# Three of seven recurrence batches on 16x16 blocks, with block layouts changed by VectorE transposes, in a fused delta-rule and SoLU kernel

## The chip, the core and the metric

The kernel runs on one core of one Trainium2 chip. The metric is the device time of a whole execution in microseconds (us), median over runs. A profiled execution also has a span, from its first to its last instruction, and a trace whose times count from the start of that span.

## The reference

A delta rule runs over 768 tokens for 4 batches times 8 heads with dimension 48; what it gives goes, row by row, through a small feed-forward layer.

```python
k_n = k / (norm(k) + 1e-6)
for t in range(S):                                   # S = 768
    kt, vt, bt = k_n[:, :, t], v[:, :, t], beta[:, :, t, None]
    y[:, :, t] = einsum('bhd,bhde->bhe', q[:, :, t], state)
    v_old = einsum('bhde,bhd->bhe', state, kt)
    state = state + bt[..., None] * einsum('bhd,bhe->bhde', kt, vt - v_old)
x = y.transpose(0, 2, 1, 3).reshape(B * S, H * D)    # 3072 x 384
h = x @ w_in                                         # 384 x 1024
solu = h * softmax(h)
ln = (solu - mean) / sqrt(var + 1e-6) * g_ln
out = ln @ w_out                                     # 1024 x 384
```

## The kernel before, in words

The 768 steps are cut into 12 chunks of 64 tokens. A **unit** is one chunk of one pair of batches (128 partitions: two batches of 64 tokens; 8 heads in the free direction). There are 24 units, worked in the order 0 to 23. Inside a chunk the 64 steps are replaced by a triangular system: with G the Gram matrix of the chunk's keys, a lower triangular matrix is inverted, and the result T (tile `zt`) is applied by TensorE. So a unit goes: `gram` and `qk` on TensorE (line 498), T ready, then the `chain` (line 649): `kps` from the state, `r` on VectorE (DVE), `ups` from T and r, `u` on ScalarE (ACT), `cps` and `yps`, the state; then `moe_h` (line 709: `h` on TensorE, softmax on DVE and ACT, tiles `pr`, `ph`, `pl`), then `moe_out` (line 759: `ops`, `oc`). Here "u of unit 10" is the ACT copy that follows the unit's `ups`.

T is made for several units at once, in seven **batches** m: m=0 has units 0 and 1, m=1 to 5 have four each (2 to 5, 6 to 9, 10 to 13, 14 to 17, 18 to 21), m=6 the last two. For a batch:

- `gram` copies G to SBUF (ACT, tile `g`) and sends it to DRAM (`gd`).
- `to_inv` reads it back with another layout into `ginv`: one partition holds one 32x32 diagonal block of one unit and head, so that 128 blocks lie side by side. `norms` takes the key norms from its diagonal (18 small DVE instructions), `inv_begin` scales it (two 128x1024 DVE instructions and a select on GpSimd, POOL), the start of the tile `y`.
- `inv_step` is the recurrence that inverts a 32x32 block: 30 steps, each one multiply (`itmp`) and one add (`y`). For m=0 and 1 a step is split: columns 0 to 9 on DVE, the rest on POOL. For m>1 all of it is on POOL. The select that opens a batch on POOL ("the select of m=3") and the last `y` bound the batch there.
- `inv_end` has ACT turn a copy of the block round and sends both through DRAM (`zd`, `xd`) into the layout that TensorE needs: `zt`, `gx` and `gy`. Eight DMAs, all in SP's queue, which also holds every other transfer.
- `block_level` puts two 32x32 blocks together to 64x64 (TensorE `mps`, ACT `msb`, TensorE, ACT).

The weights come as 8-byte numbers. `to_f32` turns them to 32-bit ones with DVE, ACT and POOL, and they are kept as a high and a low half each (`win_hi`, `win_lo`, `wout_hi`, `wout_lo`): six pieces of w_in and eight of w_out. `column_sums` (TensorE tile `cs`) needs all of w_out, and stands ahead of the first `ops` on TensorE.

The order of every engine's instructions is set when the program is built: a recorder gives every instruction a cost and a due time, runs through them once by these numbers (`order`), and emits each engine's list. An engine works its list strictly in order. For example, a DMA is costed so, and the batches' due times are written out:

```python
return self.rec.add(self.name, self.engine.dma_start, (), kw, kb * 5.0, 2000)
tn = e - 5.4 if m > 1 else -10.8
add(inversion(m, tn + 0.6, e - 2.6 if m > 1 else -10))
```

Of the kernel before, what the change touches and what calls it, by code (L numbers as in the profile page):

```python
# [305 lines left out]
def kernel(  # L306
# [190 lines left out]

    def gram(m, u, t0):
# [8 lines left out]
        if m == 2:  # L507
            rec.after = last0[0]
        for h2 in range(0, H, 2):
            with rec.atomic():  # L510
                for h, b2 in hb[2 * h2 : 2 * h2 + 4]:
                    pe.matmul(
                        ns=60, out=gps_[half(1 - b2), h], lhsT=k[dims(b2), h, 0], rhs=k[dims(b2), h, 0],
                        start=True, stop=True,
                    )
                    pe.matmul(
                        ns=60, out=pps[half(b2), h], lhsT=k[dims(b2), h, 0], rhs=k[dims(b2), h, 1],
                        start=True, stop=True,
                    )
        rec.after = None  # L520
        act.copy(out=g, in_=gps_)
# [7 lines left out]
    ginv, yt = {}, {}  # L529
    last0 = [None]  # L530

    def to_inv(m):
        gi = p2.tile([P, 32, 32], F32, tag="ginv", name=f"ginv_{m}")
        ginv[m] = gi
        for b in range(4):
            blk = b % 2
            for z in range(1 if len(units(m)) == 4 else 2):
                src = gdt[m].rearrange("t u h j -> t (u h) j")
                n = H * len(units(m))
                ls = slice(0, n)  # L540
                sp.dma_start(
                    kb=128, out=gi[32 * b + 16 * z : 32 * b + 16 * z + n],
                    in_=src[32 * b : 32 * b + 32, ls, blk * 32 : blk * 32 + 32].rearrange("j l i -> l j i"),
                )

    def inv_begin(m):
        gi, nn, nb = ginv[m], nnt[m], bb[m]
        full = [P, 32, 32]
# [12 lines left out]
    def inv_step(m, j):
        y, b = yt[m], ginv[m]
        n = 31 - j
        parts = [(gps, 0, j)] if m > 1 else [(dve, 0, min(j, 10)), (gps, 10, j)]
        for eng, c0, c1 in parts:
            if c1 <= c0:
                continue
            c = c1 - c0
            tmp = p1.tile([P, 256], F32, tag=f"itmp{eng.name}", name=f"itmp_{m}_{j}_{c0}")
            tv = tmp[:, 0 : c * n].rearrange("p (c i) -> p c i", i=n)  # L570
# [4 lines left out]
            eng.tensor_tensor(out=y[:, c0:c1, j + 1 : 32], in0=y[:, c0:c1, j + 1 : 32], in1=tv, op=ALU.add)

    def inv_end(m):
        y, x1 = yt[m], ginv[m]
# [12 lines left out]
        for b in range(4):
# [3 lines left out]
            sp.dma_start(kb=128, out=zz[rows, 0:n, blk * 32 : blk * 32 + 32], in_=zd[r0 : r0 + n].rearrange("l j i -> j l i"))  # L595
            if blk == 0:
                for t, r1 in ((xx, r0), (xy, r0 + 32)):
                    sp.dma_start(kb=128, out=t[r1 : r1 + 32, 0:n], in_=xd[r0 : r0 + n].rearrange("l j i -> j l i"))
# [328 lines left out]
```

## Time and profile before

| what | value |
|---|---|
| median of 3 runs | 512.82 us (512.18 to 515.02) |
| profiled execution, its own time | 512.04 us |
| its span | 510.2 us, mean granted TensorE clock 0.920 |
| busy: TensorE, DVE, ACT, POOL | 368.2, 318.6, 192.9, 294.0 us |
| chain that ended last | POOL 28%, PE 22%, DVE 19%, issue 10%, DMA 9%, SP's queue 7% |

The busy times are sums over the whole span. Nearly all instructions are recorded by one helper, so all have line L265, and they are told apart by tile names. In a timeline row stand the start, the duration, the engine, the tiles written and read and the shape; a row of the windows gives for a stretch of time the busy time of each engine, with the number of instructions in brackets. "SPq" is the issuing of a DMA by SP.

### The profile page before, as it was taken

How to read it: one execution, taken by the hardware profiler on the slowest of the kernel's cores; microseconds unless marked ns; L12 is line 12 of the kernel's file. 1: busy time of each engine (PE TensorE's matmuls, PEld its weight loads, DVE VectorE, ACT ScalarE, POOL GpSimd, SP SyncE). 2: the span in 40 equal slices, each digit the busy share in tenths (PEclk: the TensorE clock that was granted, in tenths of full speed). 3: DMA queues.
4: the chain of work that ended last, by engine and by line, in shares of the span. 5: the costliest groups of instructions: out<-in, count | busy, mean ns of one | idle time of the engine just before them, and what ended most of it. 6: DMA issues, size and time to landing. Idle time of an engine off the chain costs nothing.

```text
span 510.2 us, 18246 instructions
## 1 busy us (share of the span) xinstructions
PE 368.2 (72%) x7744; PEld 233.9 (46%) x7744; DVE 318.6 (62%) x791; ACT 192.9 (38%) x382; POOL 294.0 (58%) x506
## 2 busy tenths in 40 slices
PE   3510070689579488997598997787969797899974
PEld 3410070455346345665366564444635464566532
DVE  3599999887884383655088664256597355455670
ACT  2210241465522143536144544224345345454450
POOL 3378385966558998984016886008989898100000
PEclk9999999877876699998799998898989899999998
DMA  8685662987989949977999587985656866744332
GB/s 212 159 255 98 155 169 65 161 171 174 172 162 165 179 113 160 168 135 161 189 165 144 145 162 151 160 162 95 107 118 144 145 114 128 131 64 99 73 68 61
DMA packets 180640, 72.21 MB, mean 142 GB/s; under 512 B 165520, under 2 KB 168976, under 8 KB 180560
## 3 DMA queue, kind: packets, MB, share of 16 engines
q1 hardware_dynamic: 180560, 71.06, 70.8%
q8 instruction: 60, 0.98, 0.9%
q14 instruction: 20, 0.16, 0.1%
HBM read 37.21 MB, written 16.52 MB: 105 GB/s over the span
## 4 chain that ended last, share of the span: by engine, by line
POOL 28%; PE 22%; DVE 19%; issue 10%; DMA 9%; SPq 7%; ACT 4%; POOLq 0%; DVEq 0%; ACTq 0%
POOL y L265 13%; POOL itmp L265 11%; PE h L265 7%; SPq L265 7%; PE ops L265 7%; DVE y L265 5%; DVE itmp L265 4%; DMA zt<-zd 3%; DMA ginv<-gd 3%; PE mps L265 2%; DVE wf L265 2%; DVE rst L265 1%; DVE st L265 1%; PE kps L265 1%; PE yps L265 1%
## 5 line engine op out<-in xcount | busy, mean ns | idle before, releaser
L265 POOL TENSOR_TENSOR y<-y,itmp 128x84 f32<-128x84 f32 (+16 forms) x190 | 100.7, 530 | 14.6
L265 POOL TENSOR_TENSOR itmp<-y,ginv 128x84 f32<-128x84 f32 (+16 forms) x190 | 93.3, 491 | 14.0
L265 DVE TENSOR_REDUCE st<-h 128x1 f32<-128x1024 f32 x24 | 29.3, 1222 | 87.5 <-PE h L265 82.2
L265 PE MATMUL qk<-kq 48*64 48x64 f32 x768 | 40.4, 269 | 24.9 <-DVE pm L265 15.6
L265 PE MATMUL gram<-kq 48*64 48x64 f32 x768 | 43.2, 270 | 18.8 <-DMA kq<-kq_dram 11.5
L265 POOL TENSOR_TENSOR st<-st,nhalf 128x1 f32<-128x1 f32 x24 | 13.2, 551 | 64.1 <-DVE st L265 64.1
L265 PEld LDWEIGHTS gram<-kq 48*64 48x64 f32 x768 | 37.5, 178 | 25.7 <-ACT g L265 6.3
L265 PEld LDWEIGHTS <-pth 128*128 128x128 f16 x384 | 37.6, 99 | 25.5 <-issue 1.7
L265 PE MATMUL h<-win_hi,xtl 128*128 128x512 f16 x144 | 45.4, 419 | 5.3 <-DVE pr L265 2.6
L265 PE MATMUL mps<-zt,gx 32*32 32x32 f32 x768 | 13.5, 205 | 48.6 <-issue 28.9
L265 PE MATMUL h<-win_lo,xth 128*128 128x512 f16 x144 | 46.7, 421 | 1.7 <-POOL win_lo L265 1.7
L265 PEld LDWEIGHTS qk<-kq 48*64 48x64 f32 x768 | 35.8, 178 | 25.3 <-DVE pm L265 16.1
L265 PEld LDWEIGHTS <-xth 128*128 128x128 f16 x288 | 28.4, 105 | 39.7 <-issue 14.8
L265 PE MATMUL ops<-wout_hi,ptl 128*128 128x384 f16 x192 | 38.7, 345 | 8.7 <-DMA ptl<-pl 6.8
L265 PE MATMUL h<-win_hi,xth 128*128 128x512 f16 x144 | 43.4, 411 | 0.0
L265 ACT ACTIVATE e<-h,st 128x1024 f32<-128x1024 f32 x24 | 26.7, 1114 | 38.0 <-DVE st L265 26.4
L265 POOL TENSOR_SCALAR_AFFINE_SELECT y<-y 128x1024 f32<-128x1024 f32 x7 | 9.4, 1346 | 53.5 <-DVE y L265 53.5
L265 DVE TENSOR_SCALAR st<-st 128x1 f32<-128x1 f32 (+1 forms) x216 | 35.5, 165 | 5.6
L265 PE MATMUL ops<-wout_lo,pth 128*128 128x384 f16 x192 | 36.9, 334 | 0.0
L265 PEld LDWEIGHTS mps<-zt,gx 32*32 32x32 f32 x768 | 10.1, 117 | 56.9 <-issue 34.8
L265 PE MATMUL ops<-wout_hi,pth 128*128 128x384 f16 x192 | 35.5, 326 | 0.0
L265 PE MATMUL cps<-u,kv 64*64 64x48 f32 x704 | 28.9, 235 | 9.1 <-ACT u L265 3.2
(94 smaller groups left out, 860.4 us busy)
## 6 DMA issues: line engine op xcount, KB each, us to landing
kq<-kq_dram SPq DMA_DIRECT2D x48, 192.0 KB, 4.5
kv<-kv_dram SPq DMA_DIRECT2D x24, 384.0 KB, 4.3
gd<-g SPq DMA_DIRECT2D x48, 128.0 KB, 3.3
out_dram<-oc SPq DMA_DIRECT2D x24, 192.0 KB, 2.2
zd<-y SPq DMA_DIRECT2D x7, 512.0 KB, 2.6
wi<-w_in_dram SPq DMA_DIRECT2D x6, 512.0 KB, 4.4
wo<-w_out_dram SPq DMA_DIRECT2D x8, 384.0 KB, 4.0
ginv<-gd SPq DMA_DIRECT2D x20, 128.0 KB, 4.2
```

What stands on the lines that cost most here:

```text
L265: fn(*[real(a) for a in args], **{k: real(a) for k, a in kw.items()})
```

## The change

For the batches m=0, 1 and 2 (`SPLIT = 3`):

- `gram` makes three 32x32 products per head in place of one 64x64, and ACT copies G's diagonal blocks to `gc` and its lower block straight to `gx`; nothing goes to DRAM. `to_inv` is one DVE transpose of `gc` into `ginv`.
- The recurrence runs on the two 16x16 diagonal blocks of each 32x32 block: 14 steps, the upper block on DVE and the lower on POOL, at the same time.
- `inv_end` is two DVE transposes of 128x1024 (into `zt` and `gy`), a small ACT copy and POOL memsets; no DMA.
- `small_level` is new: per unit 32 plus 32 TensorE matmuls (`sps`), an ACT scaling (`ssb`), a DVE add into `zt`, two DVE transposes of 32x256 into `gx` and two ACT copies, ahead of `block_level`.

For all batches: G goes to DRAM in one DMA per unit where there were two; the last batch's blocks are read in four DMAs, not eight; the two 16-bit halves of x (`xh`, `xl`, now one tile `x`) are transposed by one DMA, not two. The recorder's cost of a DMA has a floor, and due times and precedences of the first batches are changed.

```diff
+SPLIT = 3
...
-        return self.rec.add(self.name, self.engine.dma_start, (), kw, kb * 5.0, 2000)
+        return self.rec.add(self.name, self.engine.dma_start, (), kw, max(550.0, kb * 5.0), 2000)
...
-        return self.rec.add(self.name, self.engine.dma_start_transpose, (), kw, kb * 5.0, 2000)
+        return self.rec.add(self.name, self.engine.dma_start_transpose, (), kw, max(1400.0, kb * 5.0), 2500)
...
     def gram(m, u, t0):
...
+        near = m < SPLIT
+        if near and u == 0:
+            gct[m] = p2.tile([P, 32, 32], F32, tag="y", name=f"gc_{m}")
...
+                        for r, a, b, o in ((0, lo, lo, lo), (32, up, up, lo), (32, up, lo, up)):
+                            pe.matmul(
+                                ns=25, out=gps_[C * b2 + r : C * b2 + r + 32, h, o], lhsT=kk[:, a], rhs=kk[:, b],
+                                start=True, stop=True,
+                            )
...
+            act.copy(out=gct[m][:, hs], in_=gps_[:, :, lo])
+            for r in (32, 96):
+                act.copy(out=gxt[m][0][r : r + 32, hs], in_=gps_[r : r + 32, :, up])
...
-        for b2 in range(2):
-            sp.dma_start(kb=128, out=gdt[m][half(b2), u], in_=g[half(1 - b2)])
+        sp.dma_start(kb=256, out=gdt[m][:, u], in_=g)
...
     def to_inv(m):
...
+        if m < SPLIT:
+            dve.transpose(ns=1900, out=gi.rearrange("l j i -> l i j"), in_=gct[m].rearrange("j l i -> j i l"))
...
+    def blocks(m):
+        return [(dve, slice(0, 16)), (gps, slice(16, 32))] if m < SPLIT else [(gps, slice(0, 32))]
...
     def inv_step(m, j):
-        parts = [(gps, 0, j)] if m > 1 else [(dve, 0, min(j, 10)), (gps, 10, j)]
+        for eng, q in blocks(m):
+            y, b = yt[m][:, q, q], ginv[m][:, q, q]
+            n = q.stop - q.start - 1 - j
...
     def inv_end(m):
+        if m < SPLIT:
+            xy = p1.tile([P, 1040], F32, tag="gy", name=f"gy_{m}")
+            gps.memset(xy[:, 1024:1040], 0.0)
+            act.copy(n=256, out=x1[:, 0:16, 16:32], in_=y[:, 0:16, 0:16].rearrange("p i j -> p j i"))
+            for q in (0, 16):
+                gps.memset(x1[:, q : q + 16, q : q + 16], 0.0)
+            dve.transpose(ns=1900, out=zz[:, :, 32:64].rearrange("p l i -> p i l"), in_=y.rearrange("l j i -> l i j"))
+            dve.transpose(
+                ns=1900, out=xy[:, 0:1024].rearrange("p (l i) -> p i l", i=32), in_=x1.rearrange("l j i -> l i j"),
+            )
+            return
...
+    def small_level(u, nm, zz, z0, gx, xy):
+        t = ps_f.tile([P, 2, H, 32], F32, tag="fl", name=f"sps_{nm}")
+        mps, zps = t[:, 0, :, 0:16], t[:, 1, :, 0:16]
...
+                    pe.matmul(ns=25, out=mps[r, l], lhsT=xy[r, x : x + 32], rhs=zz[r, z0 + l, 48:64], start=True, stop=True)
+        ssb = p1.tile([P, H, 16], F32, tag="msb4", name=f"ssb_{nm}")
+        act.mul(out=ssb, in_=mps, mul=-1.0)
...
+                    pe.matmul(ns=25, out=zps[r, l], lhsT=xy[r, x : x + 32], rhs=ssb[r, l], start=True, stop=True)
+        dve.tensor_tensor(out=zz[:, zs, 48:64], in0=zz[:, zs, 48:64], in1=zps, op=ALU.add)
+        for r in lanes[::2]:
+            dve.transpose(out=gx[r], in_=zz[r, zs, 32:64])
+        for r in lanes[::2]:
+            act.copy(out=zz[r, zs, 0:32], in_=zz[r, zs, 32:64])
...
-        for x, s in ((xl, "l"), (xh, "h")):
-            t = p2.tile([P, 3, P], F16, tag=f"xt{s}", name=f"xt{s}_{nm}")
-            sp.transpose(kb=96, out=t, in_=x)
-            xt[ch, bp].append(t)
+        t = p2.tile([P, 6, P], F16, tag="xt", name=f"xt_{nm}")
+        sp.transpose(kb=192, out=t, in_=x2.rearrange("p a f -> p (a f)"))
...
-        tn = e - 5.4 if m > 1 else -10.8
+        tn = e - 5.4 if m > 1 else -12.99
```

How the instructions stand now, at three places. The last number in a name only tells tiles of one name apart; those of the two kernels are counted apart.

**The end of m=0 on DVE.** Before, the last step of the recurrence (`itmp_30`) is followed by a unit's mask product `pm` and by the norms of m=1 (`rst`, `nrn`):

```order
L265 TENSOR_TENSOR itmp_29_0_612<-y_388,ginv_321 128x20
L265 TENSOR_TENSOR y_388<-y_388,itmp_29_0_612 128x10x2
L265 TENSOR_TENSOR itmp_30_0_616<-y_388,ginv_321 128x10
L265 TENSOR_TENSOR y_388<-y_388,itmp_30_0_616 128x10
L265 TENSOR_TENSOR pm_1_620<-qk_1_417,mask 128x512
L265 TENSOR_SCALAR rst_625<-ginv_553 128x32
L265 TENSOR_SCALAR nrn_627<-rst_625 128x32
```

Now, with `wf` a piece of w_in on its way to 32 bits:

```order
L266 TENSOR_TENSOR itmp_14_0_626<-y_390,ginv_317 128x14
L266 TENSOR_TENSOR y_390<-y_390,itmp_14_0_626 128x14
L266 TENSOR_TENSOR pm_0_631<-qk_0_484,mask 128x512
L266 TENSOR_SCALAR wf_0_639<-wi_0_400 128x512
L266 TENSOR_SCALAR g_sb<-g_sb 128x8
L266 SCALAR_TENSOR_TENSOR wf_0_639<-wi_0_400,wf_0_639 128x512 x2
L266 TENSOR_SCALAR wf_1_726<-wi_1_472 128x512
L266 STREAM_TRANSPOSE zt_229<-y_390 128x32x32
L266 STREAM_TRANSPOSE gy_213<-ginv_317 128x32x32
L266 TENSOR_TENSOR pm_1_745<-qk_1_645,mask 128x512
L266 STREAM_TRANSPOSE ginv_783<-gc_392 128x32x32
```

Behind the recurrence now stand a weight piece and three transposes, the third of which opens m=1.

**m=2 on POOL.** Before, its select (`y_1918`) and its 30 steps stand ahead of the remaining w_out pieces (`wg`, `wc_o`), all rows on POOL:

```order
L265 TENSOR_TENSOR wg_1657<-wg_1657,wc_o_1614 128x384
L265 TENSOR_SCALAR wc_o_1772<-wc_o_1772,g_sb 128x384
L265 TENSOR_TENSOR st_0_1267<-st_0_1267,nhalf 128x1
L265 TENSOR_TENSOR st_0_1267<-st_0_1267 128x1
L265 AFFINE_SELECT y_1918<-y_1918 128x1024
L265 TENSOR_TENSOR wg_1767<-wg_1767,wc_o_1688 128x384
L265 TENSOR_TENSOR itmp_1_0_1984<-y_1918,ginv_1770 128x30
L265 TENSOR_TENSOR y_1918<-y_1918,itmp_1_0_1984 128x30
```

Now POOL scales its half itself and does the small steps:

```order
L266 TENSOR_TENSOR wg_1983<-wg_1983,wc_o_1919 128x384
L266 TENSOR_SCALAR wc_o_2082<-wc_o_2082,g_sb 128x384
L266 MEMSET y_2265 128x16x16 x2
L266 TENSOR_TENSOR ginv_2250<-ginv_2250,nn_2294 128x16x16
L266 TENSOR_TENSOR y_2265<-ginv_2250,nb_2292 128x16x16
L266 AFFINE_SELECT y_2265<-y_2265 128x16x16 x2
L266 TENSOR_TENSOR itmp_1_16_2330<-y_2265,ginv_2250 128x14
L266 TENSOR_TENSOR y_2265<-y_2265,itmp_1_16_2330 128x14
```

POOL's share of m=2 is cut to small instructions; the other half is in DVE's list.

**The opening of m=3, on DVE, and its way back through SP's queue.** Before, m=3's `y` stands on DVE ahead of the softmax of unit 3 (`h_1_2132`) and of the `r` of unit 5 (`r_1_2529`):

```order
L265 TENSOR_TENSOR ginv_2308<-ginv_2308,nn_2417 128x1024
L265 TENSOR_TENSOR y_2431<-ginv_2308,nb_2411 128x1024
L265 SCALAR_TENSOR_TENSOR oc_0_2461<-csum,st_0_1267,ops_0_2415 128x384
L265 TENSOR_REDUCE st_1_2473<-h_1_2132 128x1
L265 TENSOR_SCALAR st_1_2473<-st_1_2473 128x1
L265 SCALAR_TENSOR_TENSOR st_1_2473<-st_1_2473 128x1
L265 TENSOR_SCALAR st_1_2473<-st_1_2473 128x1 x4
L265 SCALAR_TENSOR_TENSOR pr_1_2512,st_1_2473<-h_1_2132,e_1_2491 128x1024
L265 SCALAR_TENSOR_TENSOR oc_1_2522<-csum,st_1_1712,ops_1_2465 128x384
L265 TENSOR_TENSOR r_1_2529<-kv_1_1915,kps_1_2201 128x384
```

Now it stands behind the softmax of unit 3 (`pl_1_3201`), the small level of unit 7 (`sps_1_3205`) and the `r` of unit 6 (`r_0_3351`):

```order
L266 SCALAR_TENSOR_TENSOR pl_1_3201<-pr_1_3169,st_1_3130,ph_1_3183 128x1024
L266 SCALAR_TENSOR_TENSOR oc_0_3272<-csum,st_0_2567,ops_0_3158 128x384
L266 TENSOR_SCALAR st_1_3130<-st_1_3130 128x1
L266 RECIPROCAL nxb_3280<-nrn_3077 128x32
L266 TENSOR_TENSOR nxb_3280<-nxb_3280 128x32
L266 TENSOR_TENSOR nb_3283<-nxb_3280,bt 128x32
L266 TENSOR_SCALAR nn_3285<-nb_3283 128x32
L266 TENSOR_TENSOR ginv_2940<-ginv_2940,nn_3285 128x1024
L266 TENSOR_TENSOR zt_229<-zt_229,sps_1_3205 128x8x16
L266 STREAM_TRANSPOSE gx_1196<-zt_229 32x256 x2
L266 TENSOR_TENSOR r_0_3351<-kv_0_2104,kps_0_3238 128x384
L266 TENSOR_TENSOR y_3359<-ginv_2940,nb_3283 128x1024
```

In SP's queue, before, from m=3's `gy` to its last `zt`:

```order
L265 DMA gy_3421<-xd_3316 32x32x32
L265 DMA_TRANSPOSE xth_0_3431<-xh_0_3417 128x3x128
L265 DMA gx_2399<-xd_3316 32x32x32
L265 DMA gd_2357<-g_0_3436 64x512 x2
L265 DMA_TRANSPOSE pth_0_3464<-ph_0_3444 128x8x128
L265 DMA_TRANSPOSE xtl_0_3476<-xl_0_3459 128x3x128
L265 DMA_TRANSPOSE ptl_0_3491<-pl_0_3467 128x8x128
L265 DMA gy_3421<-xd_3316 32x32x32
L265 DMA zt_278<-zd_3296 32x32x32
```

and now:

```order
L266 DMA gy_4225<-xd_4138 32x32x32
L266 DMA zt_312<-zd_4123 32x32x32 x2
L266 DMA gx_3041<-xd_4138 32x32x32
L266 DMA gd_3607<-g_0_4252 128x512
L266 DMA_TRANSPOSE pth_0_4283<-ph_0_4260 128x8x128
L266 DMA_TRANSPOSE ptl_0_4295<-pl_0_4279 128x8x128
L266 DMA_TRANSPOSE xt_0_4326<-x_4_0_4227 128x6x128
L266 DMA gy_4225<-xd_4138 32x32x32
L266 DMA zt_312<-zd_4123 32x32x32
```

A unit's transposes still stand ahead of the last `zt`, with one transpose and one DMA fewer. From m=4 on the selects stand at the same units as before: m=4 behind the u of unit 10, m=5 between those of units 14 and 15, m=6 just ahead of that of unit 17.

More of the change, by code (lines that the diff above doesn't have):

```diff
@@ L511, in gram @@
                 for h, b2 in hb[2 * h2 : 2 * h2 + 4]:
[L512 to L521, printed above, removed]
+                    kk = k[dims(b2), h, 0]
+                    if near:
+                        for r, a, b, o in ((0, lo, lo, lo), (32, up, up, lo), (32, up, lo, up)):
[3 more added lines that the diff above has]
+                            )
+                    else:
+                        pe.matmul(ns=60, out=gps_[half(1 - b2), h], lhsT=kk, rhs=kk, start=True, stop=True)
+                    pe.matmul(ns=60, out=pps[half(b2), h], lhsT=kk, rhs=k[dims(b2), h, 1], start=True, stop=True)
+            rec.hold(pm)
+        if near:
+            hs = slice(H * u, H * u + H)
+            act.copy(out=gct[m][:, hs], in_=gps_[:, :, lo])
+            for r in (32, 96):
+                act.copy(out=gxt[m][0][r : r + 32, hs], in_=gps_[r : r + 32, :, up])
+        else:
+            act.copy(out=g, in_=gps_)
         dve.tensor_tensor(out=pm, in0=pps, in1=mask.unsqueeze(1).to_broadcast([P, H, C]), op=ALU.mult)
+        if near:
+            return
         if u == 0:
             gdt[m] = dr.tile([P, 4, H, C], F32, tag="gd", name=f"gd_{m}")
-        for b2 in range(2):
-            sp.dma_start(kb=128, out=gdt[m][half(b2), u], in_=g[half(1 - b2)])
-    ginv, yt = {}, {}
-    last0 = [None]
+        sp.dma_start(kb=256, out=gdt[m][:, u], in_=g)
+        moved[m] = rec.ops[-1]
+    ginv, yt, moved = {}, {}, {}
     def to_inv(m):
@@ L534, in to_inv @@
         ginv[m] = gi
+        if m < SPLIT:
+            dve.transpose(ns=1900, out=gi.rearrange("l j i -> l i j"), in_=gct[m].rearrange("j l i -> j i l"))
+            moved[m] = rec.ops[-1]
+            return
+        if len(units(m)) == 2:
+            rec.after = moved[m]
+            dve.memset(gi, 0.0)
+            rec.after = None
+        n = H * len(units(m))
+        src = gdt[m].rearrange("t u h j -> t (u h) j")
         for b in range(4):
             blk = b % 2
[L537 to L544, printed above, removed]
+            r = 32 * (b ^ 2)
+            sp.dma_start(
+                kb=4 * n, out=gi[32 * b : 32 * b + n],
+                in_=src[r : r + 32, 0:n, blk * 32 : blk * 32 + 32].rearrange("j l i -> l j i"),
+            )
@@ L557, in inv_begin @@
         act.copy(n=32, out=y.rearrange("p j i -> p (j i)")[:, 0 : 32 * 32 : 33], in_=nb)
-        yt[m] = y
     def inv_step(m, j):
-        y, b = yt[m], ginv[m]
-        n = 31 - j
-        parts = [(gps, 0, j)] if m > 1 else [(dve, 0, min(j, 10)), (gps, 10, j)]
[L565 to L570, printed above, removed]
+        for eng, q in blocks(m):
+            y, b = yt[m][:, q, q], ginv[m][:, q, q]
+            n = q.stop - q.start - 1 - j
+            if n <= 0:
+                return
+            tmp = p1.tile([P, 256], F32, tag=f"itmp{eng.name}", name=f"itmp_{m}_{j}_{q.start}")
+            tv = tmp[:, 0 : j * n].rearrange("p (c i) -> p c i", i=n)
@@ L621, in block_level @@
         msb = p1.tile([P, n, 32], F32, tag=f"msb{n}", name=f"msb_{nm}")
-        act.mul(out=msb, in_=mps, mul=-1.0)
+        for r in [slice(0, P)] if len(groups) > 1 else [slice(C * b2, C * b2 + 32) for b2 in range(2)]:
+            act.mul(out=msb[r], in_=mps[r], mul=-1.0)
         yield t1
@@ L641, in tlevel @@
         gx, gy = gxt[m]
-        gx, gy = (x[:, H * u : H * u + H] for x in (gx, gy))
+        gx = gx[:, H * u : H * u + H]
+        if m < SPLIT:
+            small_level(u, f"{m}_{u}", ztx[m], H * u, gx, gy)
+            yield from block_level(u, f"{m}_{u}", ztx[m], H * u, [(range(8), gx, gx, 0)], t0, t1)
+            return
+        gy = gy[:, H * u : H * u + H]
         yield from block_level(u, f"{m}_{u}", ztx[m], H * u, [(range(4), gx, gx, 0), (range(4, 8), gx, gy, 32)], t0, t1)
@@ L828 @@
     for i in range(8):
-        add(load_w_out(i, -1 + 0.05 * i, 2.1 + 0.05 * i))
+        add(load_w_out(i, -0.6 + 0.05 * i, 2.1 + 0.05 * i))
     add(once(2.49, column_sums))
```

98 lines of the change are left out of this document (60 added, 38 removed).

## The prediction

> **What bounds the kernel now.** I read the page first: the chain that ended last, then the slices.
>
> ```profile
> POOL 28%; PE 22%; DVE 19%; issue 10%; DMA 9%; SPq 7%; ACT 4%; POOLq 0%; DVEq 0%; ACTq 0%
> DVE  3599999887884383655088664256597355455670
> POOL 3378385966558998984016886008989898100000
> ```
>
> No engine carries the chain alone; a slice is 12.8 us. DVE is nearly full in slices 2 to 6 (26 to 89 us), POOL in slices 12 to 14 (153 to 191 us). So the limit changes, and I went to the timeline where it does: the opening of m=3.
>
> ```profile
> 182.93 1.36 DVE L265 TENSOR_TENSOR y<-ginv,nb 128x1024 f32<-128x1024 f32 x1
> 187.86 1.61 POOL L265 TENSOR_TENSOR kv<-kv,nrt 128x384 f32<-128x384 f32 x2
> 189.43 1.26 POOL L265 TENSOR_SCALAR_AFFINE_SELECT y<-y 128x1024 f32<-128x1024 f32 x1
> 230.46 0.35 SPq L265 DMA_DIRECT2D zd<-y  x1
> 232.95 0.34 SPq L265 DMA_DIRECT2D out_dram<-oc  x1
> 240.89 1.21 SPq L265 DMA_DIRECT2D gd<-g  x2
> 242.20 1.33 SPq L265 DMA_TRANSPOSE pth<-ph  x1
> 243.63 1.36 SPq L265 DMA_TRANSPOSE xtl<-xl  x1
> 247.03 0.60 SPq L265 DMA_DIRECT2D zt<-zd  x1
> 250.75 0.64 PE L265 MATMUL mps<-zt,gx 32*32 32x32 f32 x30 [5.44 <-DMA zt<-zd]
> 265.66 0.48 ACT L265 COPY u<-ups 128x384 f32<-128x384 f32 x1 [1.62 <-PE ups L265]
> 270.88 1.26 POOL L265 TENSOR_SCALAR_AFFINE_SELECT y<-y 128x1024 f32<-128x1024 f32 x1 [4.95 <-DVE y L265]
> ```
>
> DVE had m=3's `y` ready at 184.3; POOL took it only at 189.43, because m=2 and the two `kv` scalings were ahead of it. Then comes a chain without slack: POOL's 30 steps (41.0 us, 189.43 to 230.46), the way through DRAM (20.3 us to PE's `mps` at 250.75, where PE stood 5.44 us for the last `zt`), and 14.9 us to the u of unit 10. The select of m=4 follows that u by 5 us. So the span is 189.4 + 41.0 + 20.3 + 14.9, and 244.6 from u of unit 10 to 510.2. The last term stays, but for the merged DMAs: in both orders the selects of m=4 to 6 hang on the same units, and POOL's 30 steps of m=3 to 6 are untouched. The change is decided by when m=3's select comes.
>
> **What the change does to POOL and DVE before that select.** The recurrences alone (tile `itmp`; columns: stretch, length, DVE busy, POOL busy, clock, DMA), then all of DVE:
>
> ```profile
> 0.00:189.00 189.00, 42.46 (x120) 61.58 (x140) 0.87 0.77 160
> 144.00:189.00 45.00, 0.00 (x0) 33.94 (x60) 0.73 0.81 151
> 0.00:20.00 20.00, 8.61 (x28) 1.00 0.83 207
> 20.00:88.00 68.00, 60.10 (x154) 1.00 0.60 145
> 88.00:189.00 101.00, 73.50 (x156) 0.76 0.87 161
> 0.00:189.00 189.00, 142.21 (x336) 0.87 0.77 160
> ```
>
> The prices:
>
> ```profile
> 30.54 0.22 DVE L265 TENSOR_TENSOR itmp<-y,ginv 128x58 f32<-128x58 f32 x1
> 32.31 0.32 DVE L265 TENSOR_TENSOR itmp<-y,ginv 128x130 f32<-128x130 f32 x1
> L265 DVE TENSOR_TENSOR itmp<-y,ginv 128x210 f32<-128x210 f32 x2 | 0.9, 432 | 0.1
> L265 DVE TENSOR_TENSOR y<-ginv,nb 128x1024 f32<-128x1024 f32 x7 | 8.7, 1238 | 0.2
> L265 ACT COPY ginv<-y 128x1024 f32<-128x1024 f32 x7 | 13.8, 1972 | 50.1 <-issue 19.8 <-POOL y L265 18.5 <-DVE y L265 11.7
> L265 DVE STREAM_TRANSPOSE nrt<-nrn 128x32 f32<-128x32 f32 x7 | 1.4, 207 | 0.1
> 32.90 0.28 POOL L265 TENSOR_TENSOR itmp<-y,ginv 128x54 f32<-128x54 f32 x1
> L265 POOL TENSOR_TENSOR itmp<-y,ginv 128x240 f32<-128x240 f32 x10 | 7.0, 701 | 0.7
> 253.64 3.85 SPq L265 DMA_DIRECT2D ginv<-gd  x4
> ginv<-gd SPq DMA_DIRECT2D x20, 128.0 KB, 4.2
> ```
>
> POOL first. m=2 cost it 33.9 us of steps; now 28 steps of at most 64 elements at 0.28 are 7.8, with the scaling, memsets and selects of its own half, five passes of 256 elements at 0.70, some 11. So POOL is ready long before m=3, and DVE's `y` is what its select waits for. DVE's work up to there:
>
> - removed: the 120 instructions of m=0 and 1, −42.5; six scalings of 128x1024 become 128x256, 6 x (1.24 − 0.43) = −4.9 (0.43 from the row of 210 elements).
> - added: 3 x 28 steps of at most 64 elements x 0.21 (the 0.22 row, most are smaller) = +17.6.
> - added: nine transposes of 128x1024. The trace has none. From below 1.24, a DVE instruction of as many elements; from above 1.97, ACT's copy that turns each block round. I take 1.8, nearer the copy that strides, since DVE's small transpose (0.207) is no cheaper than its small products: 9 x 1.8 = +16.2; 11.2 to 17.7.
> - added: small levels of units 0 to 7, which stand ahead of m=3's `y`: an add (0.30, from the row of 130 elements) and two transposes of 32x256 (0.43 each, as for 210 elements): 8 x 1.16 = +9.3. If 32 partitions cost a quarter, it were 4; if a strided one costs double, 16.
> - moved: m=3's `y` behind the softmax of one more unit, an `oc` and an `r`: +4 (two 128x1024 passes of 1.24, the rest about 1.5).
>
> Sum: 142.2 − 42.5 − 4.9 + 17.6 + 16.2 + 9.3 + 4 = 141.9. DVE's load hardly falls; the halves taken from POOL's m=2 and the transposes eat what the short recurrence frees.
>
> How fast DVE gets through it: the first 20 us hold 8.6, as before (loads). The other 133.3 go at the density DVE shows where nothing bigger holds it, 60.1 of 68 us (88%, 20 to 88 us), rather than at the 73.5 of 101 (73%) of the stretch in which POOL was late anyway: 133.3 / 0.88 = 151.5, so 171.5. Two waits come on top. In m=0 DVE scales its half and then stands for POOL, which scales and selects its own (about 3.5, those five passes); the steps and unit 0's `pm` queue behind. And the norms of m=3 wait for G through DRAM, four issues (3.85) and 4.2 to land, less the small level beside it, about 6.5; `y` and POOL's select queue behind. Together 10: m=3's select at about 181, 8.4 earlier than 189.4.
>
> Covered, at nothing: the small levels' 64 matmuls per unit, about 1.3 us by the 30 `mps` in 0.64, and some four short ACT copies. PE has 91 of the 189 us free:
>
> ```profile
> 0.00:189.00 189.00, 97.60 (x2280) 0.87 0.77 160
> ```
>
> Were the cover gone at units 8 and 9, which come between the select and m=3's `mps`, it costs 2.6. POOL's memsets fall in the time it gains. SP loses all eight DMAs of m=0 to 2, which were not in m=3's way.
>
> **Behind the select.** POOL's 41.0 stays. In the way through DRAM, the rows show what stood between `zd` and the last `zt`: an `out_dram` with its wait (2.1 from the end of `zd`'s issue), now behind `xd`; two `gd`, now one (−0.6); two transposes of x, now one. That issue takes 1.36 for three 128-wide blocks and 1.33 for eight (`pth`), so size does not count and one goes whole, −1.3. 20.3 − 4.0 = 16.3. On the same chain of m=4 and m=5 one `gd` and one transpose go each, −2 each; m=6, with the last units' work over it, nothing.
>
> Span 510.2 − 8.4 − 4.0 − 4 = 493.8; with the 1.84 between span and time of that execution 495.6. It stands 0.8 below the median of the runs: **496 us**.
>
> **Rivals.** *DVE is denser, or the transposes cost 1.24:* 128.3 of work at 88% gives 165.8 + 10 = 176 (time 491); with 92% and half the waits 164.5 (480). For it: DVE has a weight piece to do whenever a step waits. *DVE is sparser:* the mean of both stretches,
>
> ```profile
> 20.00:189.00 169.00, 133.59 (x309) 0.86 0.76 154
> ```
>
> is 79%, 133.3 / 0.79 = 168.7, waits contained in it: select at 188.7, span 501.5, time 504. What I take, 88%, comes from a stretch of back-to-back recurrences; now steps on two engines, levels and softmaxes alternate.
>
> *No change:* the gain behind the select is 8, so it is lost when the select comes at 197; with what this kernel's measurement can tell, 0.5% or 2.6 us, at 195 to 200. That needs DVE at 75%: the stretch from 88 us, which had 73%, then simply has the same holdups again.
>
> *Slower: the two halves block one another.* Now DVE and POOL do their steps at the same time in all three batches. If each of DVE's 84 steps waits out a POOL step (0.28), that is +23.5: select at 204.5, time 520; it decides from a select at 200. Rows for and against:
>
> ```profile
> 178.24 0.21 DVE L265 TENSOR_TENSOR rst<-ginv,nrn 128x32 f32<-128x32 f32 x1
> 179.17 0.40 DVE L265 TENSOR_TENSOR nrn<-nrn,ginv 128x32 f32<-128x32 f32 x1
> 29.33 2.22 POOL L265 TENSOR_SCALAR wc_i<-wc_i 128x512 f32<-128x512 f32 x1
> 33.00 0.35 DVE L265 TENSOR_TENSOR itmp<-y,ginv 128x150 f32<-128x150 f32 x1
> ```
>
> For it: beside POOL's long steps the same small product takes 0.21 and then 0.40. Against: the 0.22 at 30.54 ran wholly inside POOL's `wc_i`, and when POOL's 0.28 steps set in at 32.90, DVE's next (0.35 for 150 elements) goes on in line with the 0.32 for 130 before it. The Trainium skill ("SBUF — State Buffer", section "Who interferes with whom") says that a DVE instruction with two SBUF inputs and a GpSimd instruction that reads SBUF exclude each other for the whole instruction, the second to issue waiting. By that rule this rival would be the forecast, at 520. The row inside `wc_i` speaks against a full lock, the 0.40 for part of one.
>
> **How the numbers follow.** About 496 (490 to 503): 0.49. Denser, 480 to 490: 0.25. Sparser, 503 to 509: 0.08. No change: 0.09. Blocked, slower: 0.09. Faster by over 0.5% is the first three, 0.82; within 0.5% 0.09; slower 0.09. The range for 8 in 10, 480 to 512, holds the first three; the slower case is left out above, a denser one still below.
>
> **What would show it.** The select of m=3 at 172 to 190, waiting on DVE's `y`, with POOL idle ahead of it, is the main step; at 195 or later the density was wrong. m=2 on POOL some 11 us. DVE busy 85 to 90% of 20 to 180 us. Transposes of 128x1024 between 1.24 and 1.97. DVE steps about 0.2 and POOL steps 0.21 to 0.28; DVE steps near 0.5 make the blocking rival right. From `zd` to `mps` about 16. The u of unit 10 about 253, and 240 from there to the end. The forecast is wrong, with its mechanism right, if PE or the clock fills the stretch behind unit 10: before, PE was busy 62.7 of the last 78 us,
>
> ```profile
> 432.00:510.00 78.00, 62.72 (x866) 36.41 (x866) 38.49 (x104) 32.75 (x60) 6.82 (x17) 0.98 0.43 89
> ```
>
> (columns from PE on), so an earlier start there is not passed on whole once PE has no gaps.

## The result, and the profile after

The changed kernel takes 572.05 us (median, 570.43 to 574.09), the kernel before 513.3 us on the same chip: 1.114 times as long (95% interval 1.109 to 1.119). The forecast was 496 us, with a range to 512 and a slower case at 520. None of its cases holds the time. The times are those of fast runs; of the version with 8 changes of shape per unit, below, one of two runs was slow, and its time is that of the other.

First the page of the changed kernel: the chain that ended last, and the slices of 14.2 us.

```profile
PE 50%; POOL 25%; DVE 9%; issue 8%; DMA 4%; ACT 2%; SPq 1%; POOLq 0%; DVEq 0%; ACTq 0%
PE   7989998999899577999987999969897799799983
DVE  3021558838442999396615586642869546266571
POOL 4051235739620564008880158840489889610100
```

TensorE, 22% of the chain before, now has half of it, and is nearly full in the first 13 slices (185 us), where DVE is idle for more than half of the time. Which work that is shows in the groups of instructions; behind the count stand the busy time and the mean of one in ns. The kernel before:

```profile
L265 PE MATMUL gram<-kq 48*64 48x64 f32 x768 | 43.2, 270 | 18.8 <-DMA kq<-kq_dram 11.5 <-ACT g L265 5.4 <-ACT zt L265 1.0
L265 PE MATMUL qk<-kq 48*64 48x64 f32 x768 | 40.4, 269 | 24.9 <-DVE pm L265 15.6 <-ACT g L265 7.4 <-issue 1.6
```

And the changed one:

```profile
L266 PE MATMUL qk<-kq 48*64 48x64 f32 x768 | 93.1, 274 | 0.4 <-ACT zt L266 0.2
L266 PE MATMUL gram<-kq 48*32 48x32 f32 (+1 forms) x1408 | 87.4, 240 | 11.9 <-DMA kq<-kq_dram 4.0 <-issue 2.4 <-DVE pm L266 2.4
```

The `qk` products are the same 768 records as before, 0.27 us each, yet TensorE is busy with them for 93.1 us and not 40.4. A mean of one doesn't show it: matmuls overlap, and what grew is the distance between them. The timeline of the changed kernel, within one unit:

```profile
33.67 0.42 PE L266 MATMUL gram<-kq 48*32 48x32 f32 x6
34.02 0.47 PE L266 MATMUL qk<-kq 48*64 48x64 f32 x2
34.42 0.42 PE L266 MATMUL gram<-kq 48*32 48x32 f32 x6
34.77 0.47 PE L266 MATMUL qk<-kq 48*64 48x64 f32 x2
```

Each matmul leaves two records, so this is three products of G and one of `qk`, for one head and batch. The pattern repeats every 0.75 us, 16 times per unit: 12.1 us. Before, a unit's `gram` and `qk` took 1.2 to 2.0 us where nothing held them (64 records from 30.0 to 32.0, and from 299.6 to 300.8). For the ten units of m=0 to 2 that is some 100 us more of TensorE, all of it in the opening. Who pays shows in the waits up to 257 us (us, times, longest), of the kernel before:

```profile
DVE pm L265 <- PE qk L265: 12.2, 6, 6.7
```

and of the changed one:

```profile
DVE pm L266 <- PE qk L266: 71.2, 9, 12.2
```

The timeline of the changed kernel has one of these waits, and what POOL waits for in the end:

```profile
54.97 0.69 DVE L266 TENSOR_TENSOR pm<-qk,mask 128x512 f32<-128x512 f32 x1 [12.21 <-PE qk L266]
256.95 1.26 POOL L266 TENSOR_SCALAR_AFFINE_SELECT y<-y 128x1024 f32<-128x1024 f32 x1 [8.60 <-DVE y L266]
```

The mask product `pm` stands in DVE's list ahead of recurrences, weights and norms, and waits for each unit's `qk`. So the select of m=3 comes at 256.95, not at 189.43, though DVE was busy for no more than 144.0 us up to there (windows, DVE alone):

```profile
0.00:257.00 257.00, 144.04 (x346) 0.96 0.36 91
```

Behind the select the kernel runs as before (timeline):

```profile
314.34 0.65 PE L266 MATMUL mps<-zt,gx 32*32 32x32 f32 x30 [4.51 <-DMA zt<-zd]
328.25 0.48 ACT L266 COPY u<-ups 128x384 f32<-128x384 f32 x1 [1.34 <-PE ups L266]
```

m=3's `mps` follows its select by 57.4 us (61.3 before), the u of unit 10 by 71.3 (76.2 before), and the end of the span follows that u by 241.7 (244.5 before).

### The profile page after: what moved, and what is told of

It reads as the page before. It is cut to its first block, busy times and chain, and to the rows that moved or that the text cites. A ratio compares the mean times of both kernels' runs of the same rounds, so it can differ in the third digit from the quotient of the medians.

```text
span 569.9 us, 21929 instructions
## 1 busy us (share of the span) xinstructions
PE 498.4 (87%) x9664; PEld 333.0 (58%) x9664; DVE 318.3 (56%) x795; ACT 206.8 (36%) x422; POOL 263.0 (46%) x475
## 4 chain that ended last, share of the span: by engine, by line
PE 50%; POOL 25%; DVE 9%; issue 8%; DMA 4%; ACT 2%; SPq 1%; POOLq 0%; DVEq 0%; ACTq 0%
POOL y L266 12%; PE qk L266 11%; POOL itmp L266 11%; PE gram L266 11%; PE h L266 9%; PE ops L266 6%; PE mps L266 3%; PE ups L266 3%; PE sps L266 2%; DVE st L266 2%; DMA zt<-zd 1%; PE kps L266 1%; PE yps L266 1%; PE cps L266 1%; POOL st L266 1%
## 5 line engine op out<-in xcount | busy, mean ns | idle before, releaser
L266 PE MATMUL gram<-kq 48*32 48x32 f32 (+1 forms) x1408 | 87.4, 240 | 11.9 <-DMA kq<-kq_dram 4.0
L266 PE MATMUL h<-win_hi,xt 128*128 128x512 f16 x288 | 89.9, 432 | 6.6 <-DVE pr L266 6.3
L266 PE MATMUL qk<-kq 48*64 48x64 f32 x768 | 93.1, 274 | 0.4 <-ACT zt L266 0.2
L266 PEld LDWEIGHTS gram<-kq 48*32 48x32 f32 (+1 forms) x1408 | 63.1, 141 | 35.9 <-issue 5.3
L266 POOL TENSOR_TENSOR y<-y,itmp 128x30 f32<-128x30 f32 (+16 forms) x162 | 78.2, 483 | 12.5
L266 POOL TENSOR_TENSOR itmp<-y,ginv 128x30 f32<-128x30 f32 (+16 forms) x162 | 76.6, 473 | 12.0
L266 PEld LDWEIGHTS <-xt 128*128 128x128 f16 x432 | 42.2, 106 | 59.1 <-issue 25.6
L266 PEld LDWEIGHTS qk<-kq 48*64 48x64 f32 x768 | 60.6, 166 | 11.3 <-ACT zt L266 0.6
L266 PE MATMUL h<-win_lo,xt 128*128 128x512 f16 x144 | 47.4, 428 | 0.0
L266 PE MATMUL ups<-r,zt 64*64 64x48 f32 x704 | 28.1, 234 | 9.3 <-DVE r L266 6.4
```

Of the source, the lines that this page charges most:

```text
L266: fn(*[real(a) for a in args], **{k: real(a) for k, a in kw.items()})
```

## Experiments

All ratios are to the kernel before, run beside each on the same chip (medians 514.9 to 515.6 us). Of the theories, A says that changing the shape of matmuls in turn stops TensorE; B that the small products or their place on the array are slow; C that the matmuls only fill a time that DVE and POOL set. The recorder orders the lists anew for every version, so an edit can move instructions that it does not touch. By their traces, three versions keep the lists of DVE, POOL and ACT instruction for instruction: "One shape" and "Fewer turns" those of the changed kernel, and "The turns put into the kernel before" those of that kernel. "Grouped" and "One 64x64 product" change them.

**Grouped.** Same matmuls, other order: all of a unit's `gram` first, then all `qk`.

```diff
+        if near:
+            with rec.atomic():
+                for h, b2 in hb: ...three products of gram...
-        for h2 in range(0, H, 2):
+        for h2 in range(0, H, H if near else 2):
```

> The changed kernel, but in a unit of m=0 to 2 all 48 products of G's blocks (32 columns) stand first and then all 16 of qk (64 columns), so the shape of the matmuls changes twice per unit and no longer 32 times. Theory A (each change of matmul shape stops TensorE for about 0.3 us): gram and qk of such a unit fall from 12.1 us to 2 to 3 us, the select of m=3 comes at 175 to 190 us instead of 257, and the time is that of the blind forecast's other terms, 490 to 503 us. Theory B (the 32-column products are slow themselves, or lie on the same part of the array as qk): still 8 to 12 us per unit and 560 to 575 us. Theory C (the opening is late for DVE's and POOL's lists, the matmuls only fill the time): the unit gets shorter and the time stays above 550 us.

512.57 us (0.9955, interval 0.9926 to 0.9983). The timeline, `qk` of one unit of m=2 and `gram` of the next, with the select of m=3:

```profile
60.43 1.94 PE L266 MATMUL qk<-kq 48*64 48x64 f32 x32
62.29 1.95 PE L266 MATMUL gram<-kq 48*32 48x32 f32 x96
192.72 1.26 POOL L266 TENSOR_SCALAR_AFFINE_SELECT y<-y 128x1024 f32<-128x1024 f32 x1 [10.01 <-DVE y L266]
```

3.75 us in place of 12.1, with the same 64 matmuls: the turns cost (12.1 − 3.75) / 30 = 0.28 us each. Grouping gives back 59.5 us. As it also changes the lists, it speaks against C without settling it; the versions that keep their lists do that. A was too hopeful by 1 us per unit, and the time is 10 us above its range: the select of m=3 came at 192.7, not by 190.

**One shape, more matmuls.** `qk` in two 32-column products, in turn with `gram` as in the changed kernel.

```diff
-                    pe.matmul(ns=60, out=pps[half(b2), h], lhsT=kk, rhs=k[dims(b2), h, 1], ...)
+                    for r, a in ((0, lo), (32, up)):
+                        pe.matmul(ns=30, out=pps[C * b2 + r : C * b2 + r + 32, h], lhsT=kk[:, a], rhs=k[dims(b2), h, 1], ...)
```

> The changed kernel, the order of the products as it was, but qk of m=0 to 2 is made by two products of 32 columns as well, so that all of a unit's products have one shape; TensorE gets 16 more matmuls per unit. Theory A: no stops, 80 matmuls of about 30 ns, 2 to 3 us per unit, 490 to 505 us. Theory B: 80 slow matmuls, 12 us or more per unit, 570 us or more. Theory C: above 550 us.

520.14 us (1.0109, interval 1.0035 to 1.0183). With 16 more matmuls a unit takes 2.2 to 3.8 us, not 12.1. The lists are the changed kernel's, and the time is 52 us shorter, so C falls. The turn by itself is no cost, only the turn of shapes. The time is above what A gave, again; the versions below show a part of that to be place, and the rest stays open.

**One 64x64 product for G.** On the other half of the array than `qk`, as before the change.

```diff
-                        for r, a, b, o in (...): pe.matmul(ns=25, out=gps_[C * b2 + r : ..., h, o], ...)
+                    pe.matmul(ns=60, out=gps_[half(1 - b2), h], lhsT=kk, rhs=kk, start=True, stop=True)
...
-            act.copy(out=gct[m][:, hs], in_=gps_[:, :, lo])
+            for r, o in ((0, lo), (32, up), (64, lo), (96, up)):
+                s = (r + 64) % 128
+                act.copy(out=gct[m][r : r + 32, hs], in_=gps_[s : s + 32, :, o])
```

> The changed kernel, but G of a unit of m=0 to 2 is one 64x64 product per head, on the other half of the array than qk, as in the kernel before; six ACT copies of 32 partitions in place of three copies bring its blocks into place. Theory A and B: gram and qk take 1.2 to 2.3 us per unit as before the change, ACT gains about 1 us per unit, and the time is 490 to 503 us. Theory C: above 550 us.

500.89 us (0.9723, interval 0.9665 to 0.978): faster than before, and 71 us faster than the changed kernel with the same recurrences, transposes, levels and DMAs, in lists of another order. Its groups of `gram` and `qk`:

```profile
L266 PE MATMUL gram<-kq 48*64 48x64 f32 x768 | 42.4, 267 | 33.2 <-DVE pm L266 17.1 <-DMA kq<-kq_dram 9.7 <-ACT gx L266 4.2
L266 PE MATMUL qk<-kq 48*64 48x64 f32 x768 | 38.7, 267 | 8.4 <-DVE pm L266 3.1 <-ACT gx L266 3.0 <-ACT zt L266 2.2
```

Its timeline at the select of m=3 and the u of unit 10:

```profile
172.77 1.26 POOL L266 TENSOR_SCALAR_AFFINE_SELECT y<-y 128x1024 f32<-128x1024 f32 x1 [16.34 <-DVE y L266]
258.68 0.48 ACT L266 COPY u<-ups 128x384 f32<-128x384 f32 x1 [1.46 <-PE ups L266]
```

DVE's busy time up to that select (windows):

```profile
0.00:172.80 172.80, 137.66 (x322) 0.93 0.54 125
```

Both groups are back at the busy times of before. The select of m=3 comes 16.7 us earlier than before, but the u of unit 10 only 7.0.

**The turns put into the kernel before.** No other part of the change.

```diff
+                    if m < 3:
+                        for r in (0, 32):
+                            pe.matmul(ns=30, out=gps_[C * (1 - b2) + r : C * (1 - b2) + r + 32, h],
+                                lhsT=k[dims(b2), h, 0][:, r : r + 32], rhs=k[dims(b2), h, 0], ...)
```

> The kernel before, in which only the G of m=0 to 2 is made by two products of 32 columns and all 64 rows in place of one of 64 columns, in the same place, in turn with qk's 64-column products. Theory A: about 12 us per unit (32 changes of shape of 0.3 us) instead of 1.2 to 2.3, ten units, and the time goes up by 40 to 70 us, to 550 to 580 us. Theory B, the place on the array: 513 us, no change; theory B, slow 32-column products: 32 of them at 90 ns make about 4 us per unit, 515 to 530 us. Theory C: no change.

582.33 us (1.1318, interval 1.1246 to 1.1389), 67 us more and 2 us above A's range. DVE's, POOL's and ACT's lists are those of the kernel before. Its timeline in a unit of the opening:

```profile
33.71 0.42 PE L265 MATMUL gram<-kq 48*32 48x64 f32 x4
34.06 0.47 PE L265 MATMUL qk<-kq 48*64 48x64 f32 x2
34.46 0.42 PE L265 MATMUL gram<-kq 48*32 48x64 f32 x4
```

and its waits up to the select of m=3:

```profile
DVE pm L265 <- PE qk L265: 74.9, 9, 11.9
```

Again 0.75 us from one `gram` to the next, with two products of it instead of three, on the other half of the array, and twice as wide: neither their number nor their place sets the 0.75, the two changes of shape do. B falls as the cause of the loss, and DVE waits for `qk` as in the changed kernel.

**Place.** The 64x64 version, with G on `qk`'s half of the array.

```diff
-                    pe.matmul(ns=60, out=gps_[half(1 - b2), h], lhsT=kk, rhs=kk, start=True, stop=True)
+                    pe.matmul(ns=60, out=gps_[half(b2 if near else 1 - b2), h], lhsT=kk, rhs=kk, ...)
...
-                s = (r + 64) % 128
+                s = r
```

> The version with one 64x64 product per head for G, but G on the same half of the array as qk, so that the shape never changes and only half of the array's quadrants work. Theory P (place): qk alone took 1.6 us for 16 products in the grouped version, so gram and qk take 3.3 to 4 us per unit of m=0 to 2 where the 64x64 version on both halves has 1.2 to 2.0; TensorE gets 15 to 25 us more in the opening and the time is 505 to 513 us, which would say why the grouped version stopped at 512.6 and not at 496. Rival: place is worth nothing and the grouped version lost by the order that its costs gave: 1.2 to 2.0 us per unit, 498 to 503 us.

508.92 us (0.987, interval 0.981 to 0.993). A unit takes 2.1 to 4.2 us where no load holds it; the group of `gram`:

```profile
L266 PE MATMUL gram<-kq 48*64 48x64 f32 x768 | 57.4, 271 | 25.0 <-DVE pm L266 12.8 <-DMA kq<-kq_dram 8.5 <-ACT gx L266 2.3
```

So place is worth 8 us (508.92 against 500.89, with the same lists), as the theory said; only the 1.6 us that it took for the grouped version's `qk` is 1.9 in the row shown there. The grouped version lacked 11.7 us to the 64x64 one. Place would make up most of that, if it costs as much there; the share of the lists and of the small products was not tested.

**m=2 back on 32x32**, in the 64x64 version.

```diff
-SPLIT = 3
+SPLIT = 2
```

> The version with one 64x64 product per head for G, with m=2 back on 32x32 blocks on POOL alone and through DRAM; only m=0 and 1 are on 16x16 blocks. Theory POOL: its m=2 again takes 34 to 38 us ahead of the select of m=3, which comes at 180 to 195 us instead of 172.8, time 503 to 512 us. Rival DVE: the opening is bound by DVE, which is freed of 28 steps (7 us), three transposes (6 us) and four small levels (4.6 us): select of m=3 at 160 to 172, time 490 to 500 us.

493.35 us (0.9552, interval 0.9506 to 0.9598), the fastest of all. It came out as the rival had it in the time, but not for its reason: the select of m=3 is at 176.1, 3.3 us later than with m=2 on 16x16 blocks, right behind POOL's last step of m=2, and the u of unit 10 is at 251.8, 6.9 earlier:

```profile
176.06 1.26 POOL L266 TENSOR_SCALAR_AFFINE_SELECT y<-y 128x1024 f32<-128x1024 f32 x1
251.75 0.48 ACT L266 COPY u<-ups 128x384 f32<-128x384 f32 x1 [2.40 <-PE ups L266]
```

Something between the two cost more with m=2 on 16x16 blocks.

**m=3 on 16x16 too**, in the 64x64 version.

```diff
-SPLIT = 3
+SPLIT = 4
```

> The version with one 64x64 product per head for G, with m=3 on 16x16 blocks as well. Its 41 us on POOL become some 11, and its way through DRAM goes. Theory chain: the way from the select of m=3 to the u of unit 10 (85.9 us in the 64x64 version) is recurrence and DRAM, so u of unit 10 comes 15 to 35 us earlier than 258.7 and the time is 468 to 488 us. Theory pace: from unit 8 on a unit takes some 16 us whatever T does, so the u of unit 10 comes at most 5 us earlier, and DVE has 17 us more to do: 495 to 508 us.

512.45 us (0.9935, interval 0.9909 to 0.9961). The u of unit 10 is at 257.7, 1.0 earlier than in the 64x64 version: T of m=3 was not what unit 10 waited for. The 64x64 version itself shows it. TensorE came to m=3's first `mps` there without waiting for `zt`, where in the kernel before it had stood 5.44 us (timeline of the 64x64 version):

```profile
239.90 0.45 PE L266 MATMUL mps<-zt,gx 32*32 32x32 f32 x32
```

That is the theory of the pace, but the time is above its range: the select of m=5 comes at 345.3 against 335.4.

**Both halves on DVE**, in the 64x64 version.

```diff
-        return [(dve, slice(0, 16)), (gps, slice(16, 32))] if m < SPLIT else [(gps, slice(0, 32))]
+        return [(dve, slice(0, 16)), (dve, slice(16, 32))] if m < SPLIT else [(gps, slice(0, 32))]
```

> The version with one 64x64 product per head for G, with both halves of the 16x16 recurrences on DVE, one after the other, POOL without steps in m=0 to 2. Theory: DVE and POOL stood in each other's way a little (DVE's steps 0.25 to 0.29 us on average beside POOL's); alone they take 0.20 to 0.22, and DVE has some 12 to 18 us more to do, so the select of m=3 comes 5 to 18 us after 172.8 and the time is 503 to 515 us. Rival, they blocked each other wholly: the steps fall to 0.15 or less, and the time stays at 498 to 502 us or falls.

541.65 us (1.0494, interval 1.0432 to 1.0557), above both ranges: DVE's steps took 40.9 us instead of 24.3, but the select of m=3 came 45 us later (218.2). DVE's busy time up to there (windows):

```profile
0.00:218.00 218.00, 162.79 (x436) 0.76 0.43 108
```

In the 64x64 version it was 137.7 us with 322 instructions. So 25 of the 45 us are work: the 84 more steps, and 30 other instructions that now stand ahead of the select. The other 20 us DVE stood idle; why was not tested. The steps themselves went nearly as the theory said: most of those of 50 to 56 elements took 0.21 to 0.23 with DVE alone, and 0.31 to 0.34 beside POOL. The timelines show the same: in the changed kernel DVE's steps of m=0 ran after POOL's,

```profile
57.85 0.22 DVE L266 TENSOR_TENSOR itmp<-y,ginv 128x54 f32<-128x54 f32 x1
```

and in the 64x64 version beside them, the first one beside a product of POOL that lasted to 59.70:

```profile
58.49 1.24 DVE L266 TENSOR_TENSOR itmp<-y,ginv 128x14 f32<-128x14 f32 x1
58.32 1.38 POOL L266 TENSOR_TENSOR wf<-wf,wc_i 128x512 f32<-128x512 f32 x1 [0.59 <-DVE wf L266]
62.28 0.33 DVE L266 TENSOR_TENSOR itmp<-y,ginv 128x54 f32<-128x54 f32 x1
62.26 0.28 POOL L266 TENSOR_TENSOR itmp<-y,ginv 128x50 f32<-128x50 f32 x1
```

**Fewer turns.** The changed kernel with `gram` of two heads (both batches) ahead of their `qk`: 8 changes of shape per unit.

```diff
         for h2 in range(0, H, 2):
             with rec.atomic():
-                for h, b2 in hb[2 * h2 : 2 * h2 + 4]: ...three products of gram, one of qk...
+                for h, b2 in hb[2 * h2 : 2 * h2 + 4]: ...three products of gram...
+                for h, b2 in hb[2 * h2 : 2 * h2 + 4]: ...one of qk...
```

> The changed kernel, with gram's 32-column products of two heads put together ahead of their qk, so that the shape changes 8 times per unit of m=0 to 2, between the 32 times of the changed kernel and the 2 times of the grouped one; the matmuls are the same. Theory A with the price that those two give, (12.1 - 3.75) / 30 = 0.28 us per change: 3.75 + 6 x 0.28 = 5.4 us per unit, and a time of 518 to 530 us (in proportion, 524). Rival (a fixed stop per unit, not per change): 3.8 us or 12 us per unit, 512 or 572 us.

The unit came out nearly as forecast (timeline):

```profile
107.81 0.67 PE L266 MATMUL gram<-kq 48*32 48x32 f32 x24
108.41 0.69 PE L266 MATMUL qk<-kq 48*64 48x64 f32 x8
109.03 0.67 PE L266 MATMUL gram<-kq 48*32 48x32 f32 x24
```

1.22 us from one group of `gram` to the next, 5.0 us per unit (5.4 expected), so the price is one per change: 3.75, 5.0 and 12.1 us for 2, 8 and 32. DVE's, POOL's and ACT's lists are the changed kernel's, so the order of the products alone makes the difference. The time, 510.87 us, is from one run (the profiled one took 518.95); it lies below A's range and near the grouped version's 512.57. So the step from 5.0 to 12.1 us per unit, 71 us over ten units, is worth 61 us of time, while that from 3.75 to 5.0, 12.5 us over ten units, doesn't show. It would fit a loss that sets in once TensorE's free time in the opening is used up, but one run doesn't prove that, and place cost 8 us at only 2.1 to 4.2 us per unit.

**Without 16x16 blocks**: the merged DMAs, the costs and the due times alone, with m=0 and 1 on columns split between DVE and POOL as in the kernel before.

```diff
-SPLIT = 3
+SPLIT = 0
...
+        if m >= SPLIT and m <= 1:
+            ...for eng, c0, c1 in ((dve, 0, min(j, 10)), (gps, 10, j)): the step as before...
+            return
```

> All that the change does beside the 16x16 blocks: no batch on 16x16 blocks (m=0 and 1 on columns split between DVE and POOL as before), but one DMA for a unit's G, one transpose of x, the new costs of DMAs and due times. The blind forecast took 8 us from this (4 on the way of m=3 through DRAM, 4 on those of m=4 and 5): 503 to 509 us. Rival, the queue's time was hidden: 511 to 517 us.

521.72 us (1.0119, interval 1.0096 to 1.0142): both theories missed. The select of m=3 is at 203.5 and the u of unit 0 at 97.9 (before: 189.4 and 68.5), so this order opens later without the 16x16 blocks, and the DMAs' 8 us can't be read from it.

**m=0 alone on 16x16**, in the version just shown, with m=1 split by columns.

```diff
-SPLIT = 0
+SPLIT = 1
```

> The version with one 64x64 product per head for G, and only m=0 on 16x16 blocks; m=1 on columns split between DVE and POOL as in the kernel before, m=2 on POOL. Theory POOL: with m=1's half of 32x32 steps back, POOL's m=2 comes late and the select of m=3 with it (185 to 192 us), 501 to 510 us. Theory DVE: a batch on 16x16 blocks gives DVE as much work as it takes, so that m=1 makes no difference: 490 to 497 us as with m=0 and 1 on 16x16 blocks.

498.14 us (0.9679, interval 0.9654 to 0.9703), between the two theories: select of m=3 at 182.4, 6.3 us later than with m=0 and 1, and the time 4.8 us later.

**m=2 without its small levels' matmuls.** The 64x64 version with `SPLIT = 3` again.

```diff
+        if not nm.startswith("2_"):
             ...sps, ssb, zps and the add...
```

> The version with one 64x64 product per head for G and m=0 to 2 on 16x16 blocks, in which the small levels of units 6 to 9 leave out their matmuls, ACT's scaling and DVE's add (the 16x16 block between the two halves stays unfilled there; the transposes and copies stay). Theory PE: these matmuls and their round through ACT and DVE hold up units 6 to 9, and are what makes m=2 on 16x16 blocks worse than on 32x32: u of unit 10 at 248 to 254 us instead of 258.7, time 490 to 496 us. Rival: DVE's transposes and steps of m=2 do it: u of unit 10 stays at 257 to 260, time 498 to 503 us.

493.91 us (0.9602, interval 0.9558 to 0.9646), the u of unit 10 at 249.4 (timeline):

```profile
249.43 0.48 ACT L266 COPY u<-ups 128x384 f32<-128x384 f32 x1 [1.94 <-PE ups L266]
```

The theory PE holds: these matmuls, with their round through ACT and DVE, held the units up. The windows give TensorE's busy time from 173 to 240 us, in the 64x64 version:

```profile
173.00:240.00 67.00, 60.63 (x1670) 0.92 0.63 134
```

with m=2 back on 32x32:

```profile
173.00:240.00 67.00, 54.33 (x1110) 0.93 0.76 151
```

and without the levels' matmuls of m=2:

```profile
173.00:240.00 67.00, 57.38 (x1314) 0.92 0.71 144
```

At 60.6 of 67 us there was little cover for the levels of units 6 to 9; leaving out their round over TensorE, ACT and DVE gives the 7 us that m=2 on 16x16 blocks had lost. Which of the three engines counts most was not tested, and the select of m=3 was 2.4 us earlier here too (170.4).

## Why the prediction was wrong

**The step that failed** is the paragraph "Covered, at nothing". It laid TensorE's 91 free us against the small levels' 1.3 us per unit, and never entered the other matmuls that the change edits: `gram`'s three 32-column products, in turn with `qk`. They had no term in the sum at all. With 0.28 us for each of 30 more changes of shape, and some 2 us for place and number, they cost 10 us in each of ten units, 100 us against 91 that were free; from 3.8 to 81 us TensorE did nothing but this.

The runs show it from both sides: without the turns, and with G on its old half, the changed kernel is 71 us faster; the turns alone cost the kernel before 67. With the lists of the other three engines unchanged, 8 changes of shape per unit instead of 32 made the changed kernel 61 us faster, in one run.

The Trainium skill says it: "TensorEngine Tiling (Array Packing)", section "Tiling Modes", states that changing the tiling mode, as opposed to the tile, drains TensorE. The traces agree in so far as each change between 48x32 and 48x64 products costs 0.2 to 0.3 us; no row shows the drain itself. The prediction weighed a rule on DVE and POOL and left this one out, though the diff showed shapes in turn. The kernel before changes shape between one step of a unit and the next, not 32 times within one, so no row that the prediction read gives the price; the term would have had to be an unknown one, with 32 changes in each of ten units behind it.

**What held.**

- DVE's work up to the select of m=3: forecast 141.9 us, measured 144.0 in the changed kernel, 137.7 in the 64x64 version, whose order puts 24 instructions fewer ahead of the select. There DVE was busy 85% of the time from 20 to 172.8 us. The terms, in the changed kernel: transposes of 128x1024 1.90 to 2.04 us on average by tile instead of 1.8, the 84 steps 21.3 us instead of 17.6, the add 0.29 instead of 0.30, the transposes of 32x256 0.434 instead of 0.43.
- From the select to the u of unit 10, 71.3 us against 72.2 forecast; from there to the end, 241.7 against 240.6. The 71.3 fits by offsets: the way through DRAM took 18.4 us from `zd` (295.98) to `mps`, where 16.3 was forecast, but POOL's steps took 39.0 instead of 41.0, and `mps` to u 13.9 instead of 14.9. Of the 4.0 to be won 1.9 came: the one transpose of x took 2.38 us to issue there, nearly as long as the two of the kernel before (1.21 and 1.36), though its median over the 24 units is 1.22. Why it took longer there is not shown.
- With TensorE out of the way, the select came at 172.8 (forecast 172 to 190) and the time at 500.89 (forecast 490 to 503). That it fits is partly luck. The select was 8 us earlier than the 181 of the sum: DVE's two waits (10 us) hardly showed, with 1.9 us for G of m=3 and none that the profile lists for POOL's half of m=0. And the way from the select to the u of unit 10 was 85.9 us, not 72.2, because unit 10 no longer waited for T; of that, the small levels of m=2 took 7 us that stood at nothing, 2.6 at worst. So of the 16.7 us that the select came earlier than before the change, 7.0 reached that u.

**The rivals.** The slower one, DVE and POOL blocking each other, is not what happened: DVE's steps take some 0.1 us longer beside POOL's, some 8 us at most over 84 steps and not 23.5, and DVE did its work in time in the version without the turns. The rule of the Trainium skill weighed there ("SBUF — State Buffer", section "Who interferes with whom": the second instruction waits out the first) fits the step that took 1.24 us beside POOL's long product; for steps of like size on both engines the cost was a third of a POOL step. The sign "if PE or the clock fills the stretch behind unit 10" looked for TensorE in the wrong place: it filled the stretch ahead of m=3's select.

## What to carry to other kernels

An edit that touches matmul shapes gets a term of its own, even where the matmuls get smaller: count how often the shape changes along TensorE's list and multiply by a measured price, and compare the distance between matmuls, since mean and count of the records hardly move. A share of free time is no cover until the work laid against it is complete and lies in the same stretch. When a bundle of edits loses, put the suspect alone into the old kernel as well as taking it out of the new one; here 67 and 71 us agree, and the rest of the bundle was worth 4.5% once m=2 was left out of it. Compare the lists of the other engines too: a version that reorders them tests two things at once.

## What the runs showed of the hardware

- A change between 48x32 and 48x64 matmuls costs 0.2 to 0.3 us, the same with two or three small products between, and on either half of the array.
- Products of 48x64 take nearly twice as long when `gram` and `qk` are on the same half of the array as on both halves: 3.7 us instead of 2.0 for a unit of m=2 near 60 us, and 57.4 and 54.6 us busy for `gram` and `qk` against 42.4 and 38.7, though 14 of the 24 units are alike in both.
- A DVE transpose of 128x1024 32-bit elements, changing the layout as it goes, took 1.89 to 2.10 us, some 1.6 times a DVE product of that size (1.24).
- A DVE step of 50 to 56 elements mostly took 0.21 to 0.23 us alone and 0.31 to 0.34 beside a POOL step of like size (0.28); beside a POOL product of 1.38 us a DVE step of 14 elements took 1.24.
